# A gated recurrence and a maxout FFN on one core: all step lists, PSUM rooms and second-engine steps ordered anew

## The chip, the cores and the metric

The kernel runs on one core of one Trainium2 chip. The metric is the device time of one execution in microseconds; lower is better. Five engines matter: PE (TensorE, matrix products; its weight loads are listed as PEld), DVE (VectorE), ACT (ScalarE), POOL (GpSimd) and SP (SyncE, which issues most DMA transfers). Each runs its own list of instructions in order and waits for the others by semaphores.

## The reference

The first part is a linear recurrence with a complex decay (GateLoop) over q, k, v, a_re, a_im of shape (4, 8, 768, 48): batch, heads, sequence, head size. Its output, put together as 3072 tokens of 384 features, goes into an FFN that takes the largest of three projections.

```python
mag = np.sqrt(a_re * a_re + a_im * a_im)
scale = np.minimum(mag, 0.999) / (mag + 1e-06)
a_re_n, a_im_n = (a_re * scale, a_im * scale)
for t in range(S):
    ar, ai = (a_re_n[:, :, t, :, None], a_im_n[:, :, t, :, None])
    new_re = ar * S_re - ai * S_im
    new_im = ar * S_im + ai * S_re
    kv = np.einsum('bhd,bhe->bhde', k[:, :, t], v[:, :, t])
    S_re, S_im = (new_re + kv, new_im)
    y[:, :, t] = np.einsum('bhd,bhde->bhe', q[:, :, t], S_re)
...
x = np.ascontiguousarray(attn_out.transpose(0, 2, 1, 3)).reshape(B * S, H * D)
h = np.maximum(np.maximum(x @ w1, x @ w2), x @ w3)   # w: 384 x 768
out = h @ w_out                                       # 768 x 384
```

All of it is float32.

## The kernel before

The sequence is cut into 12 groups of 64 time steps (g = 0 to 11). Each group has two halves, x and y, of two batches each. In a group the decay becomes a log magnitude and an angle, running sums of both turn the recurrence into products of matrices, and the FFN follows on the 256 tokens of the group. The first projection w1 is folded away: w2 and w3 are replaced by their differences from w1, the maximum starts at 0, and w1 goes straight to the output by the product w1 @ w_out. From group 1 on the output projection is a Strassen product with seven partial products.

There is no loop in the program. The order is written out by hand as a long text, SCHEDULE (L21), a list of 1,752 words such as `Ay:4`, "step A of half y of group 4". `program` (L1023) reads it word by word, `run` (L972) calls the helper of each, and the helper issues its instructions. The class `Bound` (L191) ties each instruction to the one before it on its engine, so every engine's own order is the order of its words in SCHEDULE; all instructions but a few stand in line 198 of the profile for that reason. Two further texts go with it:

- SLOTS (L116), 258 digits: which of four PSUM rooms (two banks each) the next result of PE gets (`banks`, L208). A step that takes a room waits until the last result in it has been read.
- OTHER (L122): the words that run on a second engine. Copies, absolute values and maxima go from ACT to DVE (`copy`, `magnitude`, `larger`), additions of whole tiles from a POOL DMA to DVE (`increase`, L243), loads of q, k, v from SP's queue to POOL's (`load_kq`, `load_v`).

The words that matter here, with the engine:

- Gates, a_re and a_im of a group: `sqr sqi lnL expw expe lne relu abs lnw expL atan` on ACT, `add mulw mulai stt xor half turn` on DVE, `Lnop addw` additions (POOL DMA or DVE), `pw` on PE in groups 0 and 1.
- Angles: `cs` (PE, running sum), `t` (ACT), `nfx nfy` (DVE), `af sa sb` (ACT), `Cdx Cdy` (POOL DMA, carry into the next group).
- Sums of the log magnitude: `sumsx sumsy F` (PE), `Enx Ekx Eqx f0..f3` (ACT).
- q and k turned and scaled: `mk mq uk uq kEn` (DVE), `tpk tpq` (PE, transposes of 16 blocks), `Kc Qc` (copies), `Q1 Q2 KB QB QG` (DVE).
- Scores and state: `A B dk` (PE), `g0..g3` (DVE), `b0 b1` (ACT), `h0 h1` (DVE).
- Output of the first part: `y` (PE), `xx xy` (copy).
- FFN: `U01 U11 U02 U12` (PE; two halves of the features, projections 2 and 3), `u..` (maximum; ACT or DVE), `S1..S4` (DVE), `P1..P7 Px Py` (PE), `r1` (ACT), `r5 r6 r7 r57 ox oy oz` (DVE), `Dx Dy Dz` (store).
- Weights at the start: `WL` loads, `Wa` to `Wg` steps that turn the stored form into float32, `T t M m` (the product w1 @ w_out), `J1..J4` (Strassen's combinations of w_out), `O` for group 0.

PE uses its 128x128 array in four ways. The whole array: `U P O pw T M`. Strips of 32 columns, four products side by side: `A B y`. Quarters of 64 rows: `dk sums cs F`. Transposes of 64 rows into 112 columns: `tpk tpq`. A product in float32 is two weight loads and two matmuls in the trace (a transpose is one of each).

`activation` (L217) loads ACT's function table anew where the next function stands in another of the two sets in use (logarithm and exponential; sine and arctangent).

Of the kernel before, what the change touches and what calls it, by code (L numbers as in the profile page):

```python
# [31 lines left out]
dkx:0 Lrx:2 Lry:2 sqr:2 add:2 atan:1 lnL:2 Wb4:0 Cdy:0 turn:1 WL5:0 Wg1:0 Wc4:0 M1:0 h1x:0 expe:2 cs:1 relu:2 g1x:0
Liy:3 expw:2 t:1 Wa5:0 abs:2 lne:2 We4:0 g2x:0 mky:0 Wf4:0 uky:0 M2:0 g3x:0 Bx:0 Wb5:0 nfx:1 Wc5:0 m1:0 Z3:0 b1x:0
tpky:0 Zh:0 uqy:0 nfy:1 b0x:0 tpqy:0 We5:0 Wg4:0 Lix:3 F:1 Kcy:0 yx:0 Lqy:1 Qcy:0 Wf5:0 xor:2 m0:0 Q2y:0 xx:0 addw:2
Q1y:0 KBy:0 WL7:0 f1:1 f0:1 QBy:0 Wg2:0 sumsx:1 Enx:1 WL8:0 half:2 Cdx:1 Ekx:1 Cdy:1 U11x:0 u11x:0 Lqx:1 lnw:2 Ay:0
Wa7:0 g0y:0 Eqx:1 expL:2 af:1 U01x:0 Wb7:0 f2:1 u01x:0 U02x:0 g1y:0 By:0 mulai:2 Wg5:0 g2y:0 Wc7:0 Wa8:0 g3y:0 We7:0
b0y:0 Lky:1 b1y:0 kEny:0 Wf7:0 sumsy:1 f3:1 yy:0 mulw:2 xy:0 sb:1 dky:0 u02x:0 stt:2 U02y:0 Lkx:1 h1y:0 Z4:0 mqx:1
atan:2 U11y:0 Lnop:2 Wb8:0 mkx:1 turn:2 sa:1 ukx:1 u11y:0 U01y:0 U12y:0 u01y:0 Eky:1 uqx:1 u02y:0 Eqy:1 cs:2 u12y:0
tpqx:1 Wc8:0 We8:0 mky:1 Eny:1 Lky:2 tpkx:1 Qcx:1 Wf8:0 t:2 Wg7:0 U21y:0 Wg8:0 U21x:0 nfy:2 nfx:2 Q1x:1 Lqx:2 mqy:1
Q2x:1 kEnx:1 uqy:1 u21y:0 U22y:0 u22y:0 u21x:0 af:2 Kcx:1 sumsx:2 F:2 Ax:1 g0x:1 g1x:1 g2x:1 Ekx:2 Enx:2 Eqx:2 Z2:0  # L40
Lvx:1 f1:2 f3:2 KBx:1 h0x:1 uky:1 tpqy:1 f2:2 Qcy:1 Q1y:1 g3x:1 Oy:0 Lvy:2 tpky:1 Q2y:1 mqx:2 Lvy:1 f0:2 Lkx:2 sa:2
sqi:3 oy:0 Lry:3 J3:0 QBx:1 dkx:1 Bx:1 sb:2 h1x:1 U12x:0 QBy:1 uqx:2 QGx:1 U22x:0 Kcy:1 KBy:1 Lrx:3 Lqy:2 u22x:0
u12x:0 Ay:1 b1x:1 g0y:1 g1y:1 g2y:1 g3y:1 b0x:1 mkx:2 sqr:3 tpqx:2 Qcx:2 By:1 yx:1 add:3 lnL:3 QBx:2 expe:3 b0y:1
sumsy:2 xx:1 Eqy:2 Eky:2 expw:3 relu:3 Q1x:2 b1y:1 QGy:1 abs:3 Ox:0 Q2x:2 Lix:4 ukx:2 ox:0 mky:2 mqy:2 Dy:0 uky:2 yy:1
addw:3 tpky:2 lne:3 kEny:1 tpkx:2 Liy:4 Lnop:3 xy:1 xor:3 half:3 Cdy:2 Kcy:2 U11:1 Cdx:2 J1:0 U01:1 Lqx:3 Lrx:4 uqy:2
lnw:3 Kcx:2 KBx:2 J2:0 expL:3 u11:1 Dx:0 Eny:2 mulw:3 mulai:3 stt:3 kEny:2 h0y:1 tpqy:2 atan:3 Lry:4 sqi:4 turn:3
Qcy:2 dky:1 h1y:1 kEnx:2 sumsx:3 u01:1 J4:0 cs:3 Eqx:3 mqx:3 Ax:2 h0y:2 Ekx:3 t:3 sqr:4 add:4 g0x:2 g1x:2 g2x:2 U12:1
Enx:3 Lrx:5 nfx:3 U02:1 lnL:4 expe:4 Q1y:2 nfy:3 expw:4 u12:1 S3:1 af:3 dky:2 g3x:2 relu:4 abs:4 addw:4 Q2y:2 F:3
u02:1 Bx:2 Ay:2 Lvx:2 sb:3 S1:1 f2:3 Lkx:3 h1y:2 f1:3 QGx:2 Lqy:3 P5:1 S2:1 P7:1 f0:3 QBy:2 g0y:2 KBy:2 g1y:2 f3:3
S4:1 lnw:4 g2y:2 P1:1 expL:4 h0x:2 P6:1 r1:1 b0x:2 b1x:2 g3y:2 r6:1 dkx:2 r5:1 r7:1 lne:4 Lry:5 sa:3 Lky:3 r57:1 h1x:2  # L50
sumsy:3 By:2 xor:4 mkx:3 b1y:2 b0y:2 Eny:3 half:4 Cdy:3 Liy:5 yx:2 xx:2 mulw:4 Eky:3 Eqy:3 Py:1 QGy:2 Px:1 P4:1 P3:1
yy:2 ukx:3 uqx:3 xy:2 oy:1 tpkx:3 tpqx:3 mky:3 h0x:3 mulai:4 Kcx:3 Lix:5 sqi:5 stt:4 Qcx:3 Lqx:4 Lky:4 P2:1 uky:3
Lnop:4 atan:4 U01:2 ox:1 u01:2 tpky:3 Lvy:3 QGx:3 Kcy:3 mqy:3 Cdx:3 uqy:3 tpqy:3 turn:4 sumsx:4 Qcy:3 Lrx:6 kEny:3
KBx:3 h0y:3 Lkx:4 Q2y:3 QBx:3 Ekx:4 Enx:4 Q1y:3 Eqx:4 cs:4 F:4 f1:4 mkx:4 t:4 sqr:5 U11:2 u11:2 Lqx:6 f3:4 Q2x:3 f2:4
Dy:1 nfx:4 Q1x:3 nfy:4 Ay:3 add:5 g0y:3 Ax:3 f0:4 g0x:3 g1y:3 g2y:3 af:4 mqx:4 xor:5 Bx:3 g3y:3 sb:4 KBy:3 U02:2 sa:4
g1x:3 U12:2 ukx:4 u02:2 S3:2 g2x:3 tpkx:4 g3x:3 Lvx:3 uqx:4 Lvy:4 lnL:5 expw:5 relu:5 Lqy:4 u12:2 expe:5 Kcx:4 tpqx:4
Qcx:4 dky:3 kEnx:3 dkx:3 S1:2 h1y:3 sumsy:4 S2:2 P5:2 h1x:3 Eqy:4 QBy:3 Dx:1 abs:5 Liy:6 addw:5 b0x:3 b1x:3 lne:5
Lnop:5 half:5 Eky:4 mky:4 Eny:4 mqy:4 Cdx:4 S4:2 Cdy:4 P1:2 P6:2 Py:2 P4:2 r1:2 yx:3 r6:2 r5:2 By:3 lnw:5 expL:5 b0y:3
mulw:5 uqy:4 h0x:4 b1y:3 mulai:5 QGy:3 Px:2 stt:5 atan:5 Lix:6 P3:2 Lry:6 xx:3 sqr:6 Liy:7 P7:2 r7:2 Lkx:5 uky:4 P2:2
tpqy:4 Lky:5 Qcy:4 r57:2 tpky:4 yy:3 sqi:6 ox:2 Lqx:5 kEnx:4 kEny:4 Lvx:4 dkx:4 oy:2 add:6 xy:3 Kcy:4 sumsy:5 turn:5  # L60
sumsx:5 h1x:4 QGx:4 Dy:2 Dx:2 Ekx:5 cs:5 Q1y:4 lnL:6 Lix:7 Eqx:5 U11:3 mkx:5 expw:6 Lvx:5 relu:6 KBx:4 Q2x:4 Enx:5
expe:6 lne:6 h0y:4 Q2y:4 mqx:5 Eky:5 U01:3 Lnop:6 abs:6 Q1x:4 u11:3 t:5 nfy:5 nfx:5 Eny:5 QBx:4 u01:3 Eqy:5 mky:5
xor:6 Ax:4 af:5 g0x:4 addw:6 sb:5 dky:4 h1y:4 sa:5 F:5 half:6 f3:5 uqx:5 g1x:4 g2x:4 lnw:6 expL:6 U12:3 u12:3 f2:5
Lrx:7 f0:5 f1:5 U02:3 tpqx:5 g3x:4 mulai:6 uky:5 tpky:5 Qcx:5 mulw:6 u02:3 Lqy:5 S1:3 Ay:4 Bx:4 S2:3 P1:3 QBy:4 sqi:7
S3:3 mqy:5 b1x:4 P5:3 Kcy:5 b0x:4 KBy:4 g0y:4 P6:3 stt:6 g1y:4 uqy:5 By:4 atan:6 yx:4 ukx:5 P7:3 g2y:4 g3y:4 Lkx:6
Lry:7 sqr:7 QGy:4 b0y:4 b1y:4 Cdy:5 Cdx:5 Q1x:5 tpkx:5 xx:4 Kcx:5 turn:6 tpqy:5 add:7 S4:3 Qcy:5 Lvx:6 r1:3 yy:4 xy:4
sumsx:6 Eqx:6 cs:6 t:6 lnL:7 r6:3 Px:3 kEnx:5 r5:3 Q2x:5 Py:3 P4:3 Enx:6 h0x:5 Ekx:6 xor:7 nfy:6 kEny:5 P2:3 U01:4
r7:3 nfx:6 expw:7 dkx:5 expe:7 lne:7 relu:7 abs:7 r57:3 addw:7 QGx:5 af:6 Lry:8 Lvy:5 h1x:5 mqx:6 sb:6 Lqy:6 u01:4
sumsy:6 QBx:5 sa:6 F:6 Liy:8 U11:4 f3:6 Eqy:6 mkx:6 Q2y:5 Eky:6 KBx:5 mqy:6 P3:3 Lky:6 Q1y:5 f1:6 uqy:6 Lrx:8 h0y:5
f0:6 oy:3 Eny:6 ox:3 Bx:5 u11:4 KBy:5 lnw:7 Ax:5 g0x:5 Ay:5 g1x:5 half:7 g2x:5 expL:7 f2:6 g3x:5 mulai:7 U02:4 g0y:5  # L70
g1y:5 g2y:5 b0x:5 g3y:5 QBy:5 b1x:5 mky:6 yx:5 ukx:6 By:5 Lvy:6 Dx:3 Cdy:6 u02:4 Cdx:6 QGy:5 mulw:7 b1y:5 uqx:6 U12:4
P1:4 S3:4 b0y:5 P7:4 stt:7 atan:7 Lqx:7 xx:5 u12:4 S1:4 tpqx:6 tpkx:6 S2:4 Kcx:6 yy:5 turn:7 Lnop:7 dky:5 Qcx:6 uky:6
Lkx:7 r1:4 sqr:8 sumsx:7 xy:5 h1y:5 cs:7 t:7 kEnx:6 Lix:8 sqi:8 P6:4 Px:4 Py:4 P5:4 P2:4 P4:4 QBx:6 Dy:3 h0x:6 add:8
lnL:8 relu:8 Q1x:6 expw:8 nfx:7 Q2x:6 Eqx:7 expe:8 S4:4 nfy:7 P3:4 tpqy:6 r6:4 KBx:6 Lqx:8 abs:8 Liy:9 r5:4 r7:4 Ekx:7
r57:4 tpky:6 ox:4 oy:4 Enx:7 af:7 dkx:6 Qcy:6 kEny:6 F:7 Dx:4 sa:7 xor:8 h1x:6 half:8 sb:7 h0y:6 Lkx:8 Dy:4 f0:7 f2:7
Q2y:6 f1:7 QGx:6 U11:5 u11:5 Cdx:7 mkx:7 U12:5 Kcy:6 u12:5 Q1y:6 Lry:9 Cdy:7 U01:5 Lrx:9 Lix:9 mqx:7 addw:8 f3:7 ukx:7
# [994 lines left out]
```

## Time and profile before

| | |
|---|---|
| runs | 552.08, 551.65, 548.6 us; median 551.65 |
| profiled execution | span 550.3 us from first to last instruction; its own time is not listed apart, the median of the runs is 1.35 us above the span |
| PE | 515.6 us busy (94%), 9,998 matmuls and as many weight loads |
| DVE | 484.8 us (88%), 735 instructions |
| ACT | 363.8 us (66%), 568, of them 50 table loads |
| POOL | 115.6 us (21%), 167 |
| DMA | 47.93 MB, mean 87 GB/s |
| mean granted PE clock | 0.978 |

A busy share is an average over the span. Where a part of it has another limit, the stretch has to be looked at by itself. An engine's wait is put down to what ended last; "issue" stands for time in which the engine waited for nothing that the profile shows. Names in a row are output<-inputs of an instruction with buffer numbers left out, x counts the instructions, us are busy time.

### The profile page before, as it was taken

To read this page: it belongs to the slowest core of one execution; us is meant where nothing else is said; L and a number is where in the kernel's file an instruction comes from. 1 tells how busy PE (TensorE), PEld (TensorE's weight loads), DVE (VectorE), ACT (ScalarE), POOL (GpSimd) and SP (SyncE) were. 2 spreads that over 40 slices of the span, in tenths; PEclk is the share of its full clock that TensorE was granted. 3 is DMA by queue.
4 is the path that set the end of the run, shared out by engine and by line. 5 is a ranking of instruction groups with operands and counts; after the bars stand their busy time and mean duration, and the time that the engine had idled before them with its cause. 6 is when DMAs were issued, how large, how long until landed. Compare 5 with 4: busy or idle time off the path is not lost.

```text
span 550.3 us, 22368 instructions
## 1 busy us (share of the span) xinstructions
PE 515.6 (94%) x9998; PEld 441.4 (80%) x9998; DVE 484.8 (88%) x735; ACT 363.8 (66%) x568; POOL 115.6 (21%) x167
## 2 busy tenths in 40 slices
...
GB/s 233 243 206 170 244 129 89 101 92 69 80 89 74 96 111 104 49 91 83 104 42 121 3 52 107 64 105 112 22 104 11 66 117 2 4 30 4 2 29 29
DMA packets 117023, 47.93 MB, mean 87 GB/s; under 512 B 103936, under 2 KB 109536, under 8 KB 116928
## 3 DMA queue, kind: packets, MB, share of 16 engines
...
q8 instruction: 78, 1.28, 0.9%
...
## 4 chain that ended last, share of the span: by engine, by line
PE 71%; DVE 10%; issue 2%; ACT 1%; DVEq 0%; ACTq 0%
PE up L198 28%; PE op L198 22%; PE y L198 6%; PE tp L198 4%; PE A L198 3%; PE dk L198 3%; PE sums L198 2%; DVE atm L198 1%; PE B L198 1%; DVE Q L198 1%; PE F L198 1%; DVE QG L198 1%; PE cs L198 1%; DVE uk L198 1%; DVE xhx L198 1%
## 5 line engine op out<-in xcount | busy, mean ns | idle before, releaser
L198 PE MATMUL up<-xhx,w 128*128 128x256 f32 x792 | 177.5, 382 | 0.0
L198 PEld LDWEIGHTS up<-xhx,w 128*128 128x128 f32 x792 | 148.6, 190 | 22.4 <-DVE g L198 2.2
L198 ACT ACT_TABLE_LOAD x50 | 64.2, 1283 | 4.4 <-issue 3.6
L198 POOL DMA_DIRECT2D ar<-nf x44 | 39.9, 1297 | 77.8 <-DVE ar L198 66.7
L198 ACT COPY atm<-B 32x128 f32<-32x128 f32 x96 | 24.5, 256 | 39.4 <-DVE atm L198 24.2
L198 PE MATMUL op<-wo,xhx 128*128 128x192 f32 (+1 forms) x220 | 49.2, 362 | 0.0
L198 DVE TENSOR_TENSOR Q<-Q,f 112x1024 f32<-112x1024 f32 (+1 forms) x48 | 45.3, 951 | 0.4 <-ACT Q L198 0.2
L198 PE MATMUL y<-atm,vb 128*32 128x64 f32 x1152 | 39.4, 221 | 2.9 <-issue 2.9
L198 PEld LDWEIGHTS op<-wo,xhx 128*128 128x128 f32 x220 | 36.7, 190 | 3.3 <-issue 0.6
L198 PEld LDWEIGHTS y<-atm,vb 128*32 128x32 f32 x1152 | 33.1, 110 | 7.3 <-issue 6.2
L198 PE MATMUL y<-QG,g 112*32 112x64 f32 x1408 | 37.3, 220 | 0.5 <-issue 0.5
L198 DVE TENSOR_TENSOR ot<-ot,op 128x192 f32<-128x192 f32 (+1 forms) x67 | 27.1, 413 | 11.0 <-PE op L198 6.2
L198 DVE TENSOR_TENSOR xhx<-xhx,up 128x768 f32<-128x768 f32 x22 | 20.9, 951 | 17.9 <-PE up L198 17.9
L198 PEld LDWEIGHTS y<-QG,g 112*32 112x32 f32 x1408 | 34.6, 110 | 0.7 <-issue 0.7
L198 PE MATMUL op<-wo,strassen 128*128 128x192 f32 x176 | 34.2, 339 | 0.1
L198 POOL DMA_DIRECT2D w<-L x8 | 9.0, 1124 | 117.4 <-ACT L L198 104.8
L198 PE MATMUL op<-w,strassen 128*128 128x192 f32 x176 | 32.8, 329 | 0.0
L198 DVE COPY_PREDICATED atm<-masko,A 128x256 f32<-128x256 uint8 x72 | 31.2, 435 | 1.2
L198 PEld LDWEIGHTS op<-wo,strassen 128*128 128x128 f32 x176 | 30.0, 196 | 2.3 <-issue 0.7
L198 PE MATMUL A<-Q,K 112*32 112x80 f32 x1536 | 30.6, 234 | 0.5 <-issue 0.5
L198 PEld LDWEIGHTS op<-w,strassen 128*128 128x128 f32 x176 | 28.9, 190 | 1.9 <-ACT ot L198 0.8
L198 PEld LDWEIGHTS A<-Q,K 112*32 112x32 f32 x1536 | 27.4, 110 | 3.6 <-issue 1.4
(156 smaller groups left out, 1114.5 us busy)
## 6 DMA issues: line engine op xcount, KB each, us to landing
...
```

The lines of the kernel that those rows point to most:

```text
L198: ins = f(*a, **kw)
```

## The change

SCHEDULE, SLOTS and OTHER are replaced; no function is touched. The new SCHEDULE has the same 1,752 words, each once, in a new order; the planner that wrote the list set a price on each change of the form in which PE's array is used. SLOTS has 258 digits again. OTHER has 58 words instead of 61: 38 leave it and 35 come in. The new text is one line shorter, so L198 of the profile becomes L197.

What the new lists hold, against the old ones:

- PE: the same 358 steps. A stretch of group 4 to 5 of either list, PE's words alone:

```text
before  sumsy:6 F:6  U11:4 P3:3  Bx:5 Ax:5 Ay:5  U02:4  yx:5 By:5  U12:4 P1:4 P7:4  tpqx:6 tpkx:6  yy:5
after   Px:3 P2:3 Py:3 P4:3  Ax:5 Bx:5  P3:3 U02:4 U11:4 U12:4  Ay:5 yx:5 By:5  P7:4 P1:4 P5:4 P6:4  tpqx:6 tpkx:6  yy:5
```

- DVE 735 to 715 instructions, ACT's table loads 50 to 41, its other work up by 18 instructions. POOL issues 156 DMA transfers instead of 120, SP 207 instead of 241.

The diff, cut to its core (both lists go on in the same way for all 12 groups):

```diff
 SCHEDULE = """
-Lix:0 sqi0:0 Zf:0 Zg:0 Lrx:0 xor0:0 sqr0:0 Liy:0 Lry:0 sqi1:0 add0:0 lnL0:0 expe0:0 expw0:0 xor1:0 lne0:0 relu0:0
...
-xor:1 Enx:0 Eqx:0 lnL:1 Wc9:0 Ekx:0 tx:0 relu:1 mkx:0 csy:0 expe:1 We9:0 nfx:0 expw:1 sumsy:0 Lix:2 ty:0 Wf9:0 abs:1
...
-u02:7 Bx:8 Ax:8 Ay:8 S1:7 sb:9 Enx:9 P5:7 af:9 QBy:8 g0x:8 sa:9 g1x:8 S2:7 g2x:8 g0y:8 P1:7 lnw:10 Lnop:10 KBy:8 g3x:8
...
-u02:11 Dy:10 S3:11 P1:11 r1:11 P2:11 S1:11 S2:11 P5:11 S4:11 P6:11 kEny:11 P3:11 r6:11 r5:11 ox:11 P7:11 P4:11 r7:11
-r57:11 Dx:11 oy:11 Dy:11 oz:11 Dz:11
+Lix:0 sqi0:0 Zg:0 Lrx:0 Liy:0 Lry:0 sqr0:0 WL0:0 add0:0 sqi1:0 xor0:0 lnL0:0 sqr1:0 expe0:0 xor1:0 expw0:0 lne0:0 Zf:0
...
+b1x:3 b0x:3 h0y:3 mqx:4 uqx:4 half:5 sumsy:4 u12:2 Eqy:4 Liy:6 dkx:3 addw:5 tpqx:4 Eny:4 Eky:4 mqy:4 KBy:3 yx:3 S3:2
...
+tpky:5 u12:3 Bx:4 KBy:4 Ay:4 Qcx:5 QBy:4 b1x:4 b0x:4 S1:3 g0y:4 yx:4 S2:3 uqy:5 Lky:6 sqi:7 g1y:4 g2y:4 g3y:4 Kcy:5
+Lrx:7 S3:3 By:4 P1:3 P5:3 Lqx:6 b0y:4 r1:3 QGy:4 stt:6 P6:3 r6:3 Q1x:5 Cdx:5 b1y:4 Lix:8 P7:3 tpkx:5 sqr:7 tpqy:5
...
+r6:11 P4:11 r5:11 r7:11 r57:11 oz:11 Dz:11 ox:11 Dx:11 oy:11 Dy:11
 """
 SLOTS = """
-0123102102030230211202102303230313212132030132101320313031210210312031023103102312301230312023023023
...
+0123201323231321001021020230132123103201013021201302130101310231230201230212130123012032103213212031
...
 """
 OTHER = set("""
-abs0:0 Lkx:0 Lqx:0 afx:0 Lvy:0 Lqy:0 Lvx:0 Wg4:0 Lqx:1 Lvx:1 Wg8:0 Lvx:2 addw:3 Lqy:3 Lkx:4 Lvx:4 abs:5 Lqx:6 Lvx:3
-addw:5 Lvx:5 abs:6 u01:3 af:5 abs:7 af:6 Lky:6 Lvx:6 Lvy:5 Kcx:6 Qcy:6 Kcy:6 af:7 Qcx:7 xx:6 Lnop:8 Lvx:7 Lky:7 xy:6
-u11:6 Lvy:8 af:8 Kcy:7 Lky:8 xy:7 Qcy:8 Lkx:10 xy:8 Qcy:9 Lky:11 Lky:10 Lvy:11 Lqx:11 Lqy:11 af:11 xx:10 Qcx:11 Qcy:11
-xy:11 u01:11 u11:11
+Lkx:0 Lvx:0 Lqx:1 Lqy:0 Lqy:1 Lvx:1 Wg8:0 Lkx:3 Lqy:2 Lkx:2 Lky:2 Lqy:3 Lvy:3 Lky:3 Lkx:4 Lky:4 Lky:5 Lvy:4 Lvx:4 Lqx:5
+Lky:6 Lqx:6 Kcx:5 Lvx:5 addw:7 Lvy:6 Lvy:5 xy:5 Lvy:7 addw:8 Lqy:8 Lky:7 Lqy:7 Lky:8 Lvx:8 Lqx:8 Qcy:8 Lkx:9 Lvx:9
+Lvy:9 Lky:10 xx:8 Lqy:10 Qcy:9 Kcx:9 Lvy:10 af:10 Lqx:10 xx:9 abs:11 Lkx:10 Lvx:10 Lkx:11 Qcy:10 Lqy:11 Lqx:11 Lky:11
+xy:11
 """.split())
```

More of the change, by code (lines that the diff above doesn't have):

```diff
@@ L32 @@
[L32 to L76, printed above, removed]
@@ new lines @@
+Liy:2 Cdx:0 mulw:1 Wf1:0 Lqx:1 M0:0 Lrx:2 Lky:0 Wa4:0 lne:1 kEnx:0 Kcx:0 Fy:0 Wb2:0 Lnop:1 Wb4:0 Eky:0 Eny:0 afy:0
+Wc2:0 mulai:1 Wg1:0 Q2x:0 Cdy:0 We2:0 f2y:0 dkx:0 f1y:0 f0y:0 stt:1 Wc4:0 Wf2:0 We4:0 Q1x:0 atan:1 M1:0 turn:1 h1x:0
+Ax:0 QBx:0 Lky:1 WL5:0 Lqy:0 Wf4:0 sby:0 say:0 f3y:0 cs:1 sqr:2 sqi:2 g0x:0 Wa5:0 add:2 Wg4:0 g1x:0 mky:0 KBx:0 t:1
+lnL:2 g2x:0 mqy:0 Z3:0 expw:2 Wb5:0 M2:0 g3x:0 relu:2 Bx:0 Wg2:0 uqy:0 Lix:3 expe:2 m1:0 tpqy:0 nfy:1 nfx:1 b0x:0 uky:0
+sumsx:1 Wc5:0 xor:2 b1x:0 yx:0 Qcy:0 abs:2 xx:0 Q2y:0 WL7:0 Lvy:1 tpky:0 Q1y:0 addw:2 We5:0 U11x:0 Ekx:1 Kcy:0 Wa7:0
```

127 lines of the change are left out of this document (83 added, 44 removed).

## The prediction

> **What bounds the kernel now.** I read the page first, then the stretches of the span, the waits of the matmul engine (PE), its chain of waits, and the DMA queues in narrow windows. The span is PE's.
>
> ```profile
> span 550.3 us, 22368 instructions
> PE 515.6 (94%) x9998; PEld 441.4 (80%) x9998; DVE 484.8 (88%) x735; ACT 363.8 (66%) x568; POOL 115.6 (21%) x167
> ...
> q8 instruction: 78, 1.28, 0.9%
> ```
>
> ```profile
> 10.00:60.00 50.00, 35.65 (x344) 21.13 (x345) 49.49 (x79) 49.19 (x75) 20.51 (x28) 0.80 0.92 220
> 60.00:120.00 60.00, 56.75 (x1306) 45.53 (x1305) 57.30 (x86) 49.91 (x85) 14.39 (x17) 1.00 0.63 121
> 120.00:412.00 292.00, 291.65 (x6104) 256.83 (x6103) 278.77 (x409) 214.25 (x321) 60.67 (x74) 1.00 0.43 81
> ...
> 426.00:450.00 24.00, 21.40 (x467) 19.44 (x460) 17.95 (x27) 11.50 (x18) 9.97 (x15) 0.93 0.39 78
> ```
>
> Stretch and length, then the busy time and instructions of PE, PEld, DVE, ACT and POOL, the granted clock, the DMA share and GB/s. Until 60 us DVE (49.49 of 50) and ACT (49.19) are full and PE waits for them; from 120 us on PE is busy 291.65 of 292, and the others follow it. One stretch breaks this, 426 to 450, where PE lost 2.6 us and the granted clock fell to 0.93. The waits say why:
>
> ```profile
> PE cs L198 <- DVE w L198: 3.7, 1, 3.7
> PE y L198 <- issue: 3.4, 3, 2.6
> PE sums L198 <- ACT E L198: 3.0, 1, 3.0
> PE cs L198 <- ACT g L198: 2.9, 1, 2.9
> ```
>
> "Issue" means that PE waited for nothing that the profile shows. I looked where these stops stand in PE's program: instructions issued up to each (PE and PEld together).
>
> ```profile
> 0.00:69.34 69.34, 44.37 (x599) 27.78 (x600) 64.82 (x113) 62.15 (x100) 30.21 (x63) 0.85 0.92 220
> 0.00:106.90 106.90, 79.79 (x1359) 57.55 (x1360) 100.16 (x168) 92.53 (x150) 41.37 (x76) 0.90 0.81 178
> 0.00:427.60 427.60, 399.65 (x8106) 337.32 (x8106) 406.71 (x616) 331.88 (x510) 106.30 (x155) 0.98 0.51 103
> ```
>
> That is 1,199, 2,719 and 16,212; with the 17, 33 and 109 instructions on PE that only wait (they stand in the built program and aren't counted as busy) 1,216, 2,752 and 16,321. Less 4, 10 and 63 times 256 this leaves 192, 192 and 193: all three stops stand at the same place of a 256-instruction block. The q8 row fits: 1.28 MB in 78 packets, 19,996 instructions by 78 is 256. So q8 brings PE's code, 256 instructions a packet, and PE ran dry three times. The longest:
>
> ```profile
> 430.41 0.25 PE L198 MATMUL y<-atm,vb 128*32 128x64 f32 x2 [2.60 <-issue]
> ```
>
> ```profile
> q8 instruction: 1, 0.02, 55.9%
> ```
>
> The second fence is the DMA queues from 427.9 to 428.0 us; there is no q8 packet from 419.6 to 427.9. PE goes on 2.4 us after this packet's start. The same for the stop at 106.9, timeline and the queues from 105.05 to 105.15:
>
> ```profile
> 107.61 0.30 PE L198 MATMUL y<-QG,g 112*32 112x64 f32 x5 [0.49 <-issue]
> ```
>
> ```profile
> q8 instruction: 1, 0.02, 58.4%
> ```
>
> 2.5 us there. How early can a packet start? In a slow passage one starts at 496.11 (first row below): 18,721 instructions and 121 waits are out, 294 short of the next such place, 19,136. I take 292 for all: the time that PE needs for these must cover the request and the 2.4 us. The two rows after it bound the shortest such passage of before that lost nothing:
>
> ```profile
> 0.00:496.11 496.11, 465.54 (x9360) 396.41 (x9361) 460.86 (x694) 360.64 (x557) 115.57 (x167) 0.98 0.47 95
> ...
> 0.00:404.65 404.65, 376.70 (x7581) 317.45 (x7582) 384.96 (x585) 312.63 (x481) 103.08 (x151) 0.97 0.53 106
> 0.00:407.86 407.86, 379.92 (x7724) 320.28 (x7728) 388.13 (x589) 315.40 (x484) 103.08 (x151) 0.97 0.53 106
> ```
>
> 289 instructions and 3 waits in 3.2 us. So a passage needs between 2.5 us (the 2.4 and something to ask) and 3.2 us.
>
> **The change part by part.** Nothing is added or taken out, so PE's streaming time stays. Five things move.
>
> (1) Changes of form. I put PE's steps into four forms: whole array (up, op, wt, wm, pw), 32-column strips (A, B, y), 64-row quarters (dk, sums, cs, F) and transposes (tp). The chain gives the price of a visit, since it lists visits of one, two and three steps:
>
> ```profile
> 198.66 1.03 PE tp L198 x32
> 199.70 1.72 PE y L198 x111
> ...
> 204.45 7.97 PE up L198 x36
> 212.42 1.25 PE A L198 x64
> 213.66 1.01 PE dk L198 x55
> 214.73 0.71 PE F L198 x58
> ...
> 285.09 11.86 PE up L198 x54
> 296.95 2.35 PE A L198 x128
> 299.60 4.08 PE up L198 x18
> ...
> 370.90 1.95 PE dk L198 x119
> ...
> 399.66 1.93 PE tp L198 x64
> ```
>
> Start, duration, records (some missing). A whole-array step alone is 11.86 - 7.97 = 3.89, a visit of one 4.08: 0.19 a visit. Likewise strips by A 1.25 - (2.35 - 1.25) = 0.15, transposes 1.03 - (1.93 - 1.03) = 0.13, quarters by dk 1.01 - (1.95 - 1.01) = 0.07. Counted along the two lists, visits go from 159 to 141: whole array 54 to 50, strips 44 to 42, quarters 33 to 28, transposes 28 to 21. Gain 4 x 0.19 + 2 x 0.15 + 5 x 0.07 + 7 x 0.13 = 2.3 us; bounds 0 and 18 x 0.19 = 3.4. So the thing that is priced is worth 0.4% here.
>
> (2) Code fetch. Gathering steps of one form puts the instruction-rich ones together. Instructions (weight load and matmul) and time of a step, from these rows: A 128 in 1.1 us, y 224 in 1.6 to 1.7, dk 128 in 0.94, F 128 in 0.7, a transpose step 32 in 0.45, B 64 in 0.27 (an estimate from A: half as many, of 32 columns instead of 80, and a little to change over); but an up step has 36 in 3.89, and a P step 16 in 1.3. Before, up and P steps stand between the rich ones; now there are runs such as "Bx:4 Ay:4 yx:4 By:4", "Ay:8 yx:8 By:8", "dkx:7 sumsy:8 dky:6 F:8 Ay:7 Bx:7". I laid the 256-instruction blocks over both lists at the place that the stops give, and took each block's 292 instructions at these rates. Before: no passage under 3.0 us, one at 3.04 (it measured 3.2), next 3.3 and 3.55. After: 18 of 76 under 3.2 us, 11 of them under 2.5; the shortest 2.03 (101 instructions of dkx:2, By:2, 127 of yx:2), the typical one 42 of B, 128 of A and 122 of y in 2.18. What is missing to 3.2 adds up to 12.2 us, to 2.9 7.6, to 2.5 3.1, to 3.5 17.9. Moving the blocks by any number of instructions leaves after at 8 to 12 us for 3.0, while before rises from nothing to as much as 9; it isn't the exact place that decides. I take 3.2, the shortest that is seen to suffice, as packets often start later than at 404 us. One of the 18 (By:0 to dky:0) lies in the start, where PE waits for ACT anyway: 12.2 - 1.1 = 11 us. PE is the engine that sets the end, so nothing hides it; DVE and ACT only get ahead.
>
> In the Trainium skill, Runtime: NRT & Kernel Launch, section "Instruction fetch mechanics", code comes in blocks of 256 instructions while the one before is run, and the cost of a block's edge is "mostly hidden"; it gives PE room for 2,048 instructions. The three stops agree with the blocks and disagree with that room: with 2,048 instructions in hand PE would not stop for the very next packet. By the page this term would be nothing, the first rival below.
>
> (3) The clock. After the 2.6 us stop, the clock of 0.93 over 24 us is 24 x 0.07 = 1.7 us of lost PE time; after the stops of 0.7 us it stayed 1.00 (60 to 120). The new stops are 0.7 to 1.2 us each, nearer to the latter, but three groups of two or three blocks follow each other closely (F:7; F:8; yx:9 to P1:8) and stop PE about 2 us together. I take one fall, 1.7 us; bounds 0 and three, 5.
>
> (4) Start and engines. 26 copies, absolute values and maxima go from DVE to ACT and 8 the other way, and ACT loads its tables 9 times less. All 9 lie behind the start (up to u21x:0 there are 9 loads on both sides), where PE covers ACT (214 busy of 292) and DVE (279): worth nothing; if PE's cover were gone, 18 steps of some 0.6 to 1.2 us less on DVE. In the start ACT's list up to u21x:0 grows by abs0:0, afx:0, f1:2 and f3:2 less t:2, about 1 us, DVE's shrinks. I take +1. If DVE is what sets the start, PE's waits for it there (3.7, and some 3 in smaller ones) could go: -7; the other bound is +3. SP gives 34 loads of q, k and v to POOL, which takes 1.0 us each (DVE gives it two additions, Wg4:0 and Lnop:8):
>
> ```profile
> L198 POOL DMA_DIRECT2D vb<-in_v_dram x24 | 19.8, 1013 | 35.5 <-PE dk L198 18.9 <-PE y L198 16.2 <-POOL vb L198 0.3
> ```
>
> That is 34 us on an engine busy 115.6 of 550. They queue behind POOL's adding transfers, which wait for ACT; each is issued well ahead of its use, so 0, with +3 if some come late.
>
> (5) The end. Before, oy and oz both stand behind P4:11; now oz and ox are issued under P4 and only oy follows: one 128x192 addition, -0.35 us.
>
> Sum on the span: 550.3 - 2.3 + 11 + 1.7 + 1 - 0.35 = 561.35. The median of the runs, 551.65, lies 1.35 above the span; on it 562.7. The late packet (2.6 + 1.7 = 4.3 us) belonged to no rich run, its 292 instructions had nearly 8 us; such a thing may or may not come again, and I leave it in.
>
> **Rivals.** Code fetch costs nothing (a larger room, or packets asked for earlier in rich runs): 551.65 - 2.3 + 1 - 0.35 = 550.0, and 545.7 if the late packet doesn't recur. For it: before shows two short stops of that kind and one stray. Against: the same place in the block thrice. Chance 0.15, of it 0.05 under 546.1.
>
> The start was DVE's: 17 DVE instructions fewer stand before u22x:0 is done, PE's waits for DVE go. Decides if DVE, not ACT, ends the early waits; -8 against my sum, 554.7, or 542.0 if the fetch is free too. The waits name both engines about equally; ACT's list up to the last early wait is the longer one. Chance 0.08, of it 0.03 faster.
>
> POOL's queue: loads of k or q behind a waiting add come late and stop PE's strip steps; two or three of 1 to 3 us bring 565 to 572. For it: such an add has waited up to 36 us for ACT. Against: PE waits for no load after 120 us. Chance 0.07.
>
> That the order doesn't do what it says: 18 of 159 visits is little, so this rival is my forecast but 2.3 us later, 565.
>
> **How the numbers follow.** Forecast 0.70, the rivals 0.15, 0.08, 0.07. 1% (5.5 us) is about what measurement can tell from no change: faster is below 546.1, slower above 557.2. Slower 0.70 + 0.07 = 0.77, faster 0.05 + 0.03 = 0.08, same 0.15. Low end: passages need 2.9 us (6.5 after the start's share), no fall of the clock, no late packet, 551.65 + 6.5 - 2.3 - 4.3 = 551.5. High end: they need 3.5 (17), three falls, a late load: 551.65 + 17 - 2.3 + 5 + 2 = 573.
>
> **What would show it.** Right: PE's waits for "issue" grow from 3.4 us to some 10 to 15 us, in y, A, F and B, in about 15 stops of 0.5 to 1.3 us, each 192 or 193 over a multiple of 256 instructions; whole-array visits keep 4.08; DVE's busy time falls by some 14 us; PE's first 120 us lose within 2 us of what they lost before. Wrong: fewer than five such stops, or a PE that waits for POOL's or DVE's tiles after 120 us.

## The result: 597.05 us after 550.58 us

After takes 597.05 us in the median (595.63 to 603.76, four runs) beside 550.58 for before on the same chip (548.6 to 552.08, four runs): a ratio of 1.087 with an interval of 1.081 to 1.093. A kernel sometimes falls into a second, slower state; the ratios leave such executions out, the medians do not. The forecast of 562.7 us had the sign, one of the two mechanisms, and a quarter of the size: 11 us were foretold, 46.5 came, and 597.05 lies 24 us above the end of the forecast range, 573. The profiled run of after is its longest (603.76 us, span 601.8).

The page of after, first lines:

```profile
span 601.8 us, 22403 instructions
...
PE 532.5 (88%) x9998; PEld 452.7 (75%) x9998; DVE 470.9 (78%) x715; ACT 363.4 (60%) x577; POOL 143.0 (24%) x203
...
q8 instruction: 78, 1.28, 0.9%
```

The work is the same (9,998 matmuls, 78 packets of code), DVE is busy 13.9 us less, and PE's share falls from 94 to 88%. The stretches of the span of after (length, then busy time and instructions of PE, PEld, DVE, ACT and POOL, granted clock, DMA share, GB/s) say where PE stands idle:

```profile
10.00:60.00 50.00, 36.66 (x342) 20.28 (x343) 45.63 (x69) 45.74 (x73) 19.18 (x28) 0.80 0.93 215
60.00:120.00 60.00, 52.66 (x1147) 43.37 (x1146) 51.83 (x82) 49.97 (x81) 19.49 (x24) 0.94 0.61 121
120.00:412.00 292.00, 268.53 (x5431) 234.42 (x5431) 240.80 (x352) 195.29 (x302) 68.17 (x86) 0.98 0.37 73
```

From 120 to 412 us PE was busy 291.65 of 292 us at full clock; now it loses 23 us there and 2% of its clock. From 60 to 120 us it loses 4 us more than before and 6% of its clock. The waits of PE in after that the view puts down to "issue":

```profile
PE dk L197 <- issue: 6.1, 4, 3.0
PE y L197 <- issue: 6.0, 7, 1.9
PE B L197 <- issue: 5.4, 3, 2.5
...
PE F L197 <- issue: 2.9, 2, 1.7
...
PE A L197 <- issue: 2.3, 1, 2.3
...
PE op L197 <- issue: 0.6, 1, 0.6
```

These are 18 waits of together 23.3 us where before had 3.9 in four (y 3.4 in three, A 0.5 in one). One of them, the stretch of the span up to it and the timeline behind it:

```profile
0.00:224.66 224.66, 189.24 (x3647) 150.52 (x3649) 198.41 (x307) 176.91 (x279) 77.04 (x119) 0.93 0.61 131
```

```profile
227.16 0.75 PE L197 MATMUL A<-Q,K 112*32 112x80 f32 x12 [2.26 <-issue]
```

3,647 + 3,649 and the 65 instructions that only wait make 7,361, which is 28 times 256 and 193: the place in a block that the prediction named. Seventeen gaps of PE in after end at that place, 16 of these waits and one more, and PE goes on 2.2 to 2.9 us after the start of the packet each time. The one more is the wait of `up` in the next fence, which the view puts down to DVE because a tile came just before: it stands at 10,689, 41 times 256 and 193. Waits that before did not have, after 120 us:

```profile
PE y L197 <- ACT xhx L197: 3.2, 1, 3.2
...
PE up L197 <- DVE atm L197: 2.5, 1, 2.5
...
PE op L197 <- ACT ot L197: 2.0, 5, 0.4
...
PE tp L197 <- DVE ot L197: 1.8, 3, 0.7
```

After 120 us the granted clock fell to 0.5 four times, at 127.6, 226.6, 322.2 and 424.6 us, three times for 3.4 us and once (226.6) for 6.8. Each fall begins in one of the four longest waits (y for ACT 3.2, A 2.3, up 2.5, B 2.5) or within 1.6 us of its end.

So there were three candidates for the 35 us that the forecast lacks: the stops for code are longer than priced (theory 1); PE runs into late tiles of DVE and ACT, whose lists are new too (theory 2); the start, which ended 12.6 us later at step yx:2 (149.9 us before, 162.5 after) where +1 was forecast (theory 3).

### The profile page after: what moved, and what is told of

Read it like the earlier page. It is cut to its first block, busy times and chain, and to the rows that moved or that the text cites. A ratio compares the mean times of both kernels' runs of the same rounds, so it can differ in the third digit from the quotient of the medians.

```text
span 601.8 us, 22403 instructions
## 1 busy us (share of the span) xinstructions
PE 532.5 (88%) x9998; PEld 452.7 (75%) x9998; DVE 470.9 (78%) x715; ACT 363.4 (60%) x577; POOL 143.0 (24%) x203
## 4 chain that ended last, share of the span: by engine, by line
PE 75%; issue 8%; DVE 6%; ACT 5%; DMA 4%; ACTq 0%; POOL 0%; DVEq 0%; SPq 0%; POOLq 0%
PE up L197 32%; PE op L197 19%; PE y L197 6%; PE A L197 4%; PE tp L197 3%; PE dk L197 3%; PE sums L197 2%; DVE xhx L197 2%; PE F L197 2%; DMA xhx<-in_moe_w_dram 1%; DMA strassen<-in_moe_w_dram 1%; PE cs L197 1%; PE B L197 1%; ACT xhx L197 1%; DVE ot L197 1%
## 5 line engine op out<-in xcount | busy, mean ns | idle before, releaser
L197 PE MATMUL up<-xhx,w 128*128 128x256 f32 x792 | 183.2, 391 | 2.5 <-DVE atm L197 2.5
L197 PEld LDWEIGHTS up<-xhx,w 128*128 128x128 f32 x792 | 153.1, 195 | 24.5 <-issue 2.6
L197 POOL DMA_DIRECT2D ar<-nf x44 | 44.1, 1446 | 55.7 <-DVE ar L197 53.1
L197 PE MATMUL op<-wo,xhx 128*128 128x192 f32 (+1 forms) x220 | 48.7, 362 | 1.3 <-DVE ot L197 0.6
L197 DVE TENSOR_TENSOR xhx<-xhx,up 128x768 f32<-128x768 f32 x22 | 21.0, 953 | 36.3 <-PE up L197 36.3
L197 DVE TENSOR_TENSOR Q<-Q,f 112x1024 f32<-112x1024 f32 (+1 forms) x48 | 45.1, 953 | 4.6 <-ACT f L197 3.4
L197 PE MATMUL y<-atm,vb 128*32 128x64 f32 x1152 | 41.4, 225 | 4.8 <-ACT xhx L197 3.2
L197 DVE TENSOR_TENSOR ot<-ot,op 128x192 f32<-128x192 f32 (+1 forms) x67 | 27.4, 415 | 23.2 <-PE op L197 12.1
L197 PE MATMUL y<-QG,g 112*32 112x64 f32 x1408 | 39.6, 222 | 5.2 <-issue 5.2
L197 ACT ACTIVATE xhx<-up 128x768 f32<-128x768 f32 x22 | 17.8, 810 | 38.6 <-PE up L197 38.5
L197 PEld LDWEIGHTS op<-wo,xhx 128*128 128x128 f32 x220 | 36.8, 190 | 5.5 <-DVE ot L197 0.9
L197 PEld LDWEIGHTS y<-atm,vb 128*32 128x32 f32 x1152 | 33.9, 112 | 9.2 <-ACT xhx L197 3.8
L197 PEld LDWEIGHTS y<-QG,g 112*32 112x32 f32 x1408 | 35.9, 111 | 6.0 <-issue 6.0
L197 ACT COPY atm<-B 32x128 f32<-32x128 f32 x96 | 24.6, 257 | 26.0 <-DVE atm L197 20.2
L197 POOL DMA_DIRECT2D w<-L x8 | 7.4, 930 | 133.1 <-ACT L L197 100.3
L197 POOL DMA_DIRECT2D k<-in_k_dram x32 | 26.0, 908 | 45.1 <-DVE uk L197 44.1
L197 ACT COPY ot<-op 128x192 f32<-128x192 f32 (+1 forms) x13 | 4.5, 346 | 52.2 <-PE op L197 52.2
L197 PE MATMUL op<-w,strassen 128*128 128x192 f32 x176 | 33.0, 331 | 1.7 <-ACT ot L197 1.2
L197 PE MATMUL op<-wo,strassen 128*128 128x192 f32 x176 | 33.0, 330 | 1.5 <-ACT ot L197 0.8
L197 POOL DMA_DIRECT2D vb<-in_v_dram x28 | 22.8, 987 | 46.5 <-PE dk L197 46.5
L197 PE MATMUL A<-Q,K 112*32 112x80 f32 x1536 | 31.8, 235 | 2.3 <-issue 2.3
```

The costliest lines, as they stand in the source:

```text
L197: ins = f(*a, **kw)
```

## The experiments

### The same order, its code blocks shifted

Tiny products at PE's very start, where it stands idle for 10.8 us, move every block of code over the steps and nothing else.

```diff
+    pad = const.tile([P, 32], FP, name="pad")
+    dve.memset(pad, 0.0)
+    room = psum.tile([P, 2, 512], FP, tag="ps3", name="pad")
+    for i in range(32):  # 8 and 64 in two others
+        mm(out=room[0:32, 0, 0:32], lhsT=pad, rhs=pad, start=True, stop=True)
     blocks = weight_blocks()
```

> The order of before, word for word, with 32 tiny products (32x32, 128 PE instructions, one wait) put at PE's very start, where PE stands idle for 10.8 us; nothing else moves, but every 256-instruction block of code now begins 129 instructions earlier in the list of steps. My theory after the result (PE's code is fetched in blocks of 256, a packet starts about 1.3 us after its room is free and not within 3.4 us of the packet before, and PE goes on 2.45 us after its start): laid over before's own list this gives 21 stops of together some 24 us (at no shift: 3 stops, 1.4 us), and the clock falls that follow stops add some 5 us: 580 us, 568 to 590. Rival 1 (what after lost came from its order itself: engine moves, POOL's queue, the start, late tiles; that stops stand at block edges is a by-product): 551 us, the 32 products being hidden in the idle start. Rival 2 (the term as I priced it in the prediction, a passage needs 3.2 us): about 10 us more than before, 561.

> The same with 8 tiny products, 32 PE instructions and one wait. Theory: 10 stops of together some 12 us and 2 to 3 us of clock: 565 us, 557 to 572, between before and the shift by 128. Rival 1: 551. Rival 2: 556.

> The control: 64 tiny products, 256 PE instructions and one wait, so that every block begins (but for that one wait) at the same instruction of the steps as in before. Theory: stops as in before, 1 to 5 us together: 551 us, 549 to 555. If the cost in the two shifted kernels came from the added products themselves (time at the start, the room, a clock that they change), this one has most of them and should be the slowest of the three.

> The order of after with the same 128 instructions at its start. Theory: after's instruction-rich runs are longer than a block, so no place of the blocks frees it: 19 stops of together 22 us against 22 of 24 without: 597 us less 0 to 6, 590 to 600. Rival 1: 597. If after is only badly placed against its blocks, as before would be by a shift, a shift by half a block should bring it down by 10 us or more.

Measured, beside a before of 551.16: shift by 32 559.85 us (ratio 1.016, 1.012 to 1.020), by 128 572.24 (1.038, 1.034 to 1.043), by 256 553.06 (1.0035, 1.0012 to 1.0058); after shifted by 128 593.59 (1.076, 1.072 to 1.081), 3.5 under after itself, with intervals that just touch. PE's waits after 120 us in before shifted by 128, then one of its stops as stretch and timeline:

```profile
PE y L198 <- issue: 4.7, 3, 2.0
PE F L198 <- issue: 3.1, 4, 1.6
PE A L198 <- issue: 2.9, 3, 1.5
PE dk L198 <- issue: 2.5, 3, 1.2
```

```profile
0.00:443.41 443.41, 407.76 (x8232) 343.63 (x8234) 409.46 (x618) 333.27 (x511) 106.55 (x155) 0.97 0.50 100
```

```profile
445.66 0.26 PE L198 MATMUL y<-atm,vb 128*32 128x64 f32 x1 [2.02 <-issue]
```

8,232 + 8,234 and 111 that wait are 16,577, again 193 over a multiple of 256. In the program's steps this is 127 instructions further on, in the same y step in which before had its longest stop; most of the other stops stand in steps where before had none. The shift by 256 has one wait for issue after 120 us:

```profile
PE y L198 <- issue: 2.1, 1, 2.1
```

Rival 1 falls: with not one step moved, the place of the blocks alone costs 21 us. Before stood at a lucky place, a shift by 32 instructions takes 9 us; after is not much better off at another one. My rule for packets overshot (29 and 14 us above before, measured 21 and 9), the old price of 3.2 us a passage (rival 2) gave 10 and 5, too little for both.

### How fast code comes when nothing else runs

```diff
     program(SCHEDULE, 0)
+    room = psum.tile([P, 2, 512], FP, tag="ps0", name="tail")
+    for i in range(1024):
+        o = 32 * (i % 4)
+        mm(out=room[o:o + 32, 0, 0:32], lhsT=ident[:, 0:32], rhs=ident[:, 0:32], start=True, stop=True)
```

In two variants some of the products read weights, and loads from q into these weights follow as soon as they are read.

> Before with 1,024 products of 128x32 by 128x32 put behind its last step, in four strips in turn: 4,096 PE instructions, 16 blocks of code, while no other transfer runs. It measures by itself how fast code comes. Theory: packets start at least 3.3 to 3.4 us apart however early room is free, so PE stops at each block edge and the 16 blocks take 16 x 3.4 = 54 us (52 to 58), one stop each, PE going on about 2.45 us after the packet's start. If a passage needs no more than 2.5 us, as the low bound of the prediction had it, 40 us; if code comes as fast as PE takes it, 16 x 256 x 5 ns = 20 to 25 us without a stop.

> The same tail, and every 128 products (two blocks) PE's progress sets free two loads of 96 KB from q, into weights that are no longer used. Theory (a code packet is asked for in the same DMA engines as the data and starts later where data stand before it): the blocks with loads take 1 to 4 us longer, together 8 to 30 us above the quiet tail. If code has its own way and only the spacing counts: the same 54 us within 2.

> The tail of 4,096 PE instructions behind before's last step again; this time two bursts of eight loads of 96 KB are set free by PE's progress, one issued by SP at the tail's block 4, one by POOL at its block 10. Single pairs of loads cost nothing measurable (3.77 us a block with them, 3.65 without). Theory: a code packet that is asked for while a long burst of data stands in the DMA engines starts 2 to 6 us late, so one or two blocks of each burst take 6 to 9 us and the tail 4 to 12 us more than the quiet one (605). If code does not wait behind data at all: 605 within 2, and what delays packets in after must be something else, their own spacing.

The quiet tail adds 54.7 us (605.32 beside 550.67 in one run each), as expected. Its timeline, and its waits:

```profile
549.87 1.30 PE L198 MATMUL tail<-ident 128*32 128x32 f32 x128 [0.83 <-issue]
553.62 1.30 PE L198 MATMUL tail<-ident 128*32 128x32 f32 x128 [2.45 <-issue]
557.09 1.94 PE L198 MATMUL tail<-ident 128*32 128x32 f32 x128 [2.17 <-issue]
```

```profile
PE tail L198 <- issue: 26.1, 15, 2.4
```

128 matmuls of the trace (64 products) and as many weight loads are 256 instructions, one block: PE takes it in 1.3 to 1.9 us (at a granted clock of 0.59 from 545 to 600 us), then waits. From the packet at 547.52 us to the one at 598.63 there are 14 intervals, 3.65 us in the mean (3.43 to 3.90). So a rich run that lasts costs here 3.65 us for every 256 instructions, two to three times what PE needs for them. The variants were run once each. With pairs of loads the whole kernel took 609.8 us and an interval 3.77, with bursts 605.33 and 3.87. The tails alone, from their first matmul to their last, took 55.0 us (quiet), 56.8 (pairs) and 58.1 (bursts): the pairs stay within the 2 us of "only the spacing counts", the bursts lie between their two expectations. The longest interval inside a burst is 4.42 us, beside 3.90 in the quiet tail; one of 4.45 came before the first burst. The theory that packets wait for microseconds behind data falls: a burst costs a packet some 0.5 us.

By the Trainium skill, Runtime: NRT & Kernel Launch, section "Instruction fetch mechanics", the refill in 16 KiB blocks runs beside execution and a block's edge is "mostly hidden"; the rows agree with the block of 256 and not with the hiding, 15 edges cost 26.1 us here.

### The engines' lists

```diff
 OTHER = set("""
-Lkx:0 Lvx:0 Lqx:1 Lqy:0 Lqy:1 Lvx:1 Wg8:0 Lkx:3 Lqy:2 Lkx:2 Lky:2 Lqy:3 Lvy:3 Lky:3 Lkx:4 Lky:4 Lky:5 Lvy:4 Lvx:4 Lqx:5
...
+abs0:0 Lkx:0 Lqx:0 afx:0 Lvy:0 Lqy:0 Lvx:0 Wg4:0 Lqx:1 Lvx:1 Wg8:0 Lvx:2 addw:3 Lqy:3 Lkx:4 Lvx:4 abs:5 Lqx:6 Lvx:3
...
```

> After with the list of words for the second engine taken from before: the 26 copies, absolute values and maxima that went from DVE to ACT go back, the loads of q, k and v return to the queues they had in before; the order stays after's. Theory (the order of PE's steps and the start's order make the loss, not the engines): 597 us, 592 to 602. Rival, POOL's queue and ACT's extra work: 585 or less. If DVE is needed more than I think, 605 or more.

> After's order with before's list for the second engine, once more, for one look at its waits in the same call as the two others: 615 us as before (608 to 621); 597 would mean that the first result was chance.

615.33 us (1.112, 1.105 to 1.120), and 611.99 when the same kernel ran once more (label after_ob_half). Neither my figure nor the rival's, but the third case that was written down, 605 or more: giving the words back makes after slower by 15 to 18 us. The engine list of after fits its order, and nothing here says that the loads on POOL slow it. The run moves copies and loads together, so the loads by themselves are not tested.

### Starts and rests joined

Before's first 565 words with after's order behind them, and the reverse; PSUM rooms are dealt out anew where the two orders differ.

```diff
 # b565_a against before, at the seam
-... Liy:5 yx:2 xx:2 mulw:4 Eky:3 Eqy:3 Py:1 QGy:2 Px:1 P4:1 P3:1 yy:2 ...
+... Liy:5 yx:2 xx:2 mulw:4 Eky:3 Eqy:3 Lvx:3 Lvy:3 Lnop:4 mqy:3 Lix:5 QGy:2 Py:1 Px:1 mulai:4 ...
 # a565_b against after, at the seam
-... mulw:4 yx:2 Lix:5 sb:3 QGy:2 Py:1 Px:1 mulai:4 r57:1 ukx:3 P4:1 xx:2 P2:1 ...
+... mulw:4 yx:2 Lix:5 sb:3 h0y:2 dky:2 h1y:2 r57:1 xx:2 Py:1 QGy:2 Px:1 P4:1 ...
```

> The first 565 words as in before (until yx:2, which before reached at 149.9 us and after at 162.5), all words after them in after's order, with after's second engines from there on; PSUM rooms given out anew by the same rule of lifetimes. Theory: the 12.6 us that after is late at yx:2 go, the rest keeps its stops: 597 - 12.6 = 584.5 us, 577 to 590. If the late start is made up later anyway, or comes from what the start hands on (loads, tables): 597. If the whole loss sat in the start: 551.

> The reverse: the first 565 words as in after, the rest in before's order, so that the blocks of code lie over the rest as in before to within a few instructions. Theory: 551 + 12.6 = 563.8 us, 559 to 570, with the few stops that before has from there on. If the code fetch explains all (no other cost in the start than its stop of 3.2 us): 555. If after's start spoils what follows: above 570.

After's start with before's rest takes 570.17 us (1.034, 1.030 to 1.037): the start, with the join, costs 19 us, more than the 12.6 it is late by. Before's start with after's rest has a median of 601.1 us and a ratio of 1.082 (1.076 to 1.088), no clear gain over after's 1.087. So the two parts do not add up, and theory 1 needed a test that leaves the order alone.

### Rich runs broken up in after

Up and P steps are put between the instruction-rich ones again, by a search with the packets' rule as its price; the second kernel moves steps of all forms.

```diff
 # PE's words alone, a stretch of group 7
-U02:6 sumsx:8 dkx:7 sumsy:8 dky:6 F:8 Ay:7 Bx:7 U12:6 P1:6 ... P3:6 P2:6 yy:7 tpkx:8
+sumsx:8 dkx:7 U02:6 sumsy:8 dky:6 F:8 Ay:7 U12:6 Bx:7 P1:6 ... P3:6 yy:7 P2:6 tpkx:8
```

> After's order with 37 of PE's steps at other places: from word 409 on, up and P steps are moved by at most six PE steps so that they stand between A, y, dk and F steps again and no passage of 292 instructions is short; the other engines' lists are after's word for word, the rooms too but for two. This is the opposite of what the change does: visits of a form rise from 141 to 164, which costs 4 us by the chain's prices. Theory: by the rule of packets (asked for 1.3 us after room is free, 3.4 us apart, PE on 2.45 us after the start) PE's stops fall from 24 us to 8; with a third of that again in clock, less 4 us for the visits, 597 - 17 = 580 us, 572 to 590. Rival 1, changes of form are what counts and the stops are a side show: 601. Rival 2, the other engines' lists make the loss: 597 within 3.

> The same with steps of all forms allowed to move (43 PE steps at other places, 168 visits, all rooms as in after). Theory: stops 5 us instead of 24, 597 - 20 = 577 us, 568 to 588. Rival 1: 602. Rival 2: 597.

607.93 us (1.102, 1.098 to 1.107) and 610.0 (1.103, 1.096 to 1.110): slower than after by 11 and 13 us, where theory 1 had 17 to 20 less. Most of the stops did go: PE's waits for issue after 120 us are 8.7 us in the first and 5.7 in the second, where after has 19.7. The longest waits of the second after 120 us:

```profile
PE op L196 <- DVE ot L196: 3.3, 3, 1.8
PE op L196 <- ACT K L196: 2.7, 2, 2.0
PE up L196 <- DVE atm L196: 2.7, 1, 2.7
PE up L196 <- ACT f L196: 2.6, 1, 2.6
PE y L196 <- ACT xhx L196: 2.5, 1, 2.5
PE dk L196 <- issue: 2.1, 2, 1.1
```

In place of "issue" stand waits for tiles, most of them at up and P steps (op), the kind that was moved. My reading, not tested by itself: a step put earlier comes ahead of its tile, one put later makes ACT and DVE late, since each runs its list in order. A search that prices code alone lost elsewhere here. It also left theory 2 alive.

### Half the instructions, the same order

A, y and dk issue half as many products of twice the width, so that a step streams about as long with half the instructions. Every second product is left out and its place is taken by the wider one, so these kernels serve to measure time and are no remedy.

```diff
-            for h in range(H):
+            wide = ps.rearrange("p a (b t) -> p a b t", b=HU)
+            for h in range(0, H, 2):
                 for o in range(0, P, 32):
-                    mm(out=ps[o:o + 32, h // HU, h % HU * P:h % HU * P + 80], lhsT=T["K", x][0:DD, h, o:o + 32],
-                       rhs=T["Q", x][0:DD, 4 * h + o // 32], start=True, stop=True)
+                    mm(out=wide[o:o + 32, h // HU, h % HU:h % HU + 2, 0:80], lhsT=T["K", x][0:DD, h, o:o + 32],
+                       rhs=T["Q", x][0:DD, 4 * h + o // 32:4 * h + o // 32 + 2], start=True, stop=True)
...
-                        mm(out=ps[lo:hi, j, n * D:(n + 1) * D], ...
+                        mm(out=ps[lo:hi, j, n * D:n * D + P], ...   # dk, n = 0, 2, 4, 6
...
-                for c in range(2):
+                for c in range(1):                                   # y, both halves' columns at once
```

> The control for the next one: before, where A, y and dk issue half as many products of twice the width (A 32 of 160 columns, y 56 of 128, dk 32 of 128 where they had 64 of 80, 112 of 64, 64 of 48), so that each step streams about as long as before with half the PE instructions. The values of these three are not the reference's any more: every second product is left out and its place filled by the wider one. No passage of 292 instructions is short then, wherever the blocks lie. Every theory: before has next to no stops as it is, so 549 us, 545 to 553.

> After with the same halving; its order, rooms and second engines are untouched, and each step streams about as long as before. Theory 1 (stops for code and the clock falls behind them are the larger part of the loss, the start the rest): the stops go, 25 to 28 us with 7 us of clock, and what stays above the control is the start's 12.6 and some small waits: 565 us, 558 to 573. Theory 2 (what after_broken suggests: with the stops gone PE only runs into late tiles of DVE and ACT, because after's lists for those engines do not keep up): 590 us or more.

Before falls to 548.75 us (0.993, 0.990 to 0.997), after to 568.73 (1.029, 1.025 to 1.034): the distance between the two goes from 46.5 us to 20.0. (The before run beside these two took 551.98.) Theory 2's 590 is out, theory 1's 565 is missed by 4, inside its 558 to 573. The stretches of halved before, then of halved after:

```profile
57.00:101.00 44.00, 39.34 (x630) 30.34 (x630) 42.88 (x66) 38.57 (x64) 14.78 (x16) 1.00 0.75 144
...
220.00:320.00 100.00, 99.92 (x1525) 87.38 (x1525) 95.64 (x142) 67.13 (x107) 20.75 (x26) 1.00 0.36 68
```

```profile
57.00:101.00 44.00, 38.24 (x608) 31.30 (x608) 36.56 (x57) 35.83 (x62) 19.07 (x22) 0.88 0.71 136
...
220.00:320.00 100.00, 96.37 (x1472) 84.35 (x1467) 88.05 (x133) 74.92 (x114) 27.01 (x34) 1.00 0.40 76
```

The clock of after is back at 1.00 in its middle, so its fall there belonged to the stops. Some 4 us in 100 are still lost there, to small waits for DVE and ACT, and in the start 57 to 101 us goes at a clock of 0.88 where halved before has 1.00.

### The two starts and rests without code fetch

The joined kernels, with the same halving.

> After's first 565 words and before's order behind them, with A, y and dk halved as in before_half (every second product left out, the others twice as wide), so that code fetch plays no part. It prices after's start by itself. At yx:2 after_half was 9.8 us later than before_half: 548.75 + 9.8 = 558.5 us, 556 to 562. If the start is made up later: 550. If the start explains all that is left of after's loss: 568.

> Before's first 565 words and after's order behind them, halved too. Theory (start and rest add up): 568.73 - 9.8 = 559 us, 555 to 563. If after's rest waits for DVE, ACT or POOL however early PE comes to it, as b565_a (601, no gain) suggests: 566 to 570.

| | before's rest | after's rest |
|---|---|---|
| before's start | 548.75 | 575.81 |
| after's start | 564.9 | 568.73 |

Each stands beside a before of 551.8 to 552.0. With before's rest, after's start costs 16.2 us (that kernel's ratio to before is 1.024, 1.022 to 1.026), above my 9.8: the lateness at yx:2 grows behind the join. After's own rest then adds 3.8, little beside intervals that overlap (halved after has 1.025 to 1.034). Taken the other way round, the same table says something else: after's rest behind before's start costs 27.1 us, and after's start in front of it makes the kernel 7.1 us faster. Part of this is the join, since the joined lists do not meet: one wait of 4.7 us stands right at the seam, where PE's step P3:1 waits for an addition that DVE has behind other work, and the granted clock is 0.69 from 156 to 167 us. That is some 8 us of the 27.1; the rest gathers behind it, in waits of up to 2.4 us and one more fall of the clock. So the split of the 20.0 us into start and rest depends on the order in which they are taken, and only the sum is firm.

```profile
PE op L194 <- DVE ot L194: 6.3, 3, 4.7
```

### Two additions on DVE instead of POOL

What costs time in the start? The chain of waits of a565_b_half has this piece, with start and duration:

```profile
103.36 15.95 issue
...
119.32 4.02 DMA w<-L
...
123.42 0.84 ACT L L194
124.29 0.48 ACT ot L194
124.77 0.39 ACT xhx L194
125.21 1.92 PE y L194 x37
```

Addition addw:3 is on DVE in before and an adding transfer of POOL in after; ACT waits for it, and the copy that y needs stands behind it on ACT. ACT's waits for such transfers in before, in halved after, and in the kernel of the next lines, which puts two additions on DVE, addw:3 as before had it and addw:2:

```profile
ACT L L198 <- DMA w<-L: 0.9, 1, 0.9
```

```profile
ACT L L197 <- DMA w<-L: 8.9, 3, 4.4
```

```profile
ACT L L197 <- DMA w<-L: 7.4, 2, 5.1
```

```diff
 OTHER = set("""
-Lkx:0 Lvx:0 Lqx:1 Lqy:0 ...
+addw:2 addw:3 Lkx:0 Lvx:0 Lqx:1 Lqy:0 ...
```

> After_half with two additions of the start, addw:2 and addw:3, on DVE instead of POOL's adding transfers (before had addw:3 there). In after_half ACT waits 8.9 us in three stops for such transfers before the logarithm that follows them, in before_half next to nothing, and the copy that PE's y step of half y of group 1 needs stands behind one of them. If these waits set the start's loss: 568.7 less 4 to 7, 562 to 565. If they only pass on a lateness that comes from the weights and the clock, or DVE's two additions of 0.9 us cost what they save: 567 to 570.

566.04 us (1.026, 1.023 to 1.028), 2.7 under halved after, with intervals that overlap: between the two expectations, and ACT still waits 7.4 us for others. These additions are a small part of the start's loss at most, and none is shown clear of noise. The rest of it stays open: the weights' staging and the lower clock stand beside it, but no run here took either away.

## Why the prediction was right in sign and wrong in size

Two steps failed. The price of a passage in (2), 3.2 us as enough for 292 instructions, was too low, and with the clock of (3) the term came to 26.5 us instead of 12.7. The start in (4), +1 us from comparing sums of work, should have been some 10 to 16.

- The sign, and why: right. PE stops for code where instruction-rich steps stand together, always 192 or 193 over a multiple of 256; forecast about 15 stops, seen 17; forecast 18 short passages. By an estimate at the prediction's own rates, 14 of the 17 stand at a passage under 3.2 us; the other three (3.6, 4.1 and 8.3 us) had a late packet, so the close count is luck in part. Shifting blocks, the tail and the halving each show the mechanism.
- (1) Changes of form, -2.3: nothing contradicts it. A whole-array step alone still takes 4.08 us and a visit of two 7.97:

```profile
146.79 4.08 PE up L197 x18
...
188.56 7.97 PE up L197 x36
```

  No run priced it by itself; what it is worth is buried under ten times as much.
- (2) Code fetch, +11 with 1.7 of clock as (3): this is the step that failed most. Halving takes 28.3 us off after and 1.8 off before (550.58), so code and the clock behind it are worth 26.5, against 12.7. The count was near, the price of a stop was not: 0.5 to 1.3 us were forecast, 0.4 to 3.0 came. I took 3.2 us as enough for 292 instructions because one passage of before had that and lost nothing; it was a lucky one, not a typical one. Its packet started 0.5 us after its room was free (counted as in the prediction, 292 instructions ahead), where the median over before's packets is 1.5 us. In a quiet tail a packet already comes only every 3.65 us, and in after the packets at stops started 0.9 to 4.7 us after their room was free (one 9.2), where 3.2 less the 2.4 to go on leaves 0.8. What makes them later than 0.9 us, beyond their own spacing, stays open. It is not data alone: in the tails a burst cost some 0.5 us, and the packet that was 9.2 us late started at 386.03 us in after, when the DMA queues had carried no packet at all from 380 to 386. On the prediction's own list of passages, by its own rates, 21 are short of 3.65 us by 21 us together, 25 are short of 4 by 29 (estimates). The prediction had 17.9 for 3.5 as its upper bound; taking one lucky passage as the measure made the range too narrow as well. The rival that the fetch costs nothing is refuted by the shifts.
- (3) The clock, one fall of 1.7: too few. It stands at 0.98 over 292 us in after, 5.8 us, and at 1.00 in the middle once the stops are taken out. I had the pattern right (a fall behind a stop of 2.6 us) and the stops too short: three of 2.3 to 2.5 us came after 120 us, each with its fall. The fourth fall stands behind a wait of 3.2 us for ACT, which belongs to (4).
- (4) Start and engines, +1 with +3 as a bound: wrong by about 9 to 15. At yx:2 after is 12.6 us late and halved after 9.8; with before's rest behind it the halved start costs 16.2. The sign that PE's first 120 us lose within 2 us of what they lost before failed too: by the rows above and the prediction's they lost some 3 us of busy time and, at a clock of 0.94 over 60 us, 3.6 more. I compared sums of work on ACT and DVE up to one step. The chain above goes through a transfer, ACT and PE in turn, and no sum of one engine's list shows that. Which link costs the time was not settled.
- Loads on POOL, 0: not contradicted; with them (and the rest of the list) back after is slower, and they were not moved by themselves. The rival of POOL's queue had the wrong words: ACT's long waits in halved after are for adding transfers (8.9 us in three), not for the loads.
- The sign of being wrong, a PE that waits for POOL's or DVE's tiles after 120 us, came in a small way: seven waits for DVE of 0.2 to 0.7 us, 3.8 us together (the 2.5 at `up` is a stop for code), and ACT's besides.
- (5) The end, -0.35: too small to be seen.
- Added up: code and clock 26.5, start and rest together 20.0, is the 46.5 us. The 26.5 is shown. The 20.0 divides into 16.2 and 3.8 in one order of taking them only; with code fetch in play the start alone costs 18.8.
